# The order of TensorE's work inside one attention step: first half of the scores ahead of the turns

## The chip, the cores and the metric

The kernel runs on one core of a Trainium2 chip. The metric is the time of one execution on the device, in microseconds (us); lower is better. The engines are named as in the profile: PE is TensorE (PEld its weight loads), DVE is VectorE, ACT is ScalarE, POOL is GpSimd, SP is the queue that issues most transfers.

## The reference

Three stages follow one another, all in float32:

```python
# 1. attention with a top-32 mask: 4 batches, 8 heads, 576 rows, head size 64
scores = scale * np.matmul(q, k.transpose(0, 1, 3, 2))
kth = np.partition(scores, -32, axis=-1)[..., -32:-31]
scores = np.where(scores >= kth, scores, -1e9)
attn = np.exp(scores - scores.max(-1, keepdims=True))
x = (attn / (attn.sum(-1, keepdims=True) + 1e-9)) @ v      # 2304 tokens x 512
# 2. a gated layer, 512 -> 1536 -> 512
x = (x @ w_a * (x @ w_b)) @ w_out
# 3. eight experts 512 -> 1024 -> 512; each token goes to one, by cosine similarity
out[mask_e] = gate[mask_e] * (np.maximum(x[mask_e] @ w1[e], 0.0) @ w2[e])
```

## The kernel before, in words

**Tiles and parts.** Attention is cut into 144 tiles of 128 query rows by 576 keys. A part is a pair of heads of one batch and some of its rows, of 1, 4 or 5 tiles; there are 36 parts. The first part of a batch and head pair is called a lead part: it also brings in and turns its keys.

**One tile.** PE computes the scores in two halves of 288 columns (`scores`, matmul L373), and ACT copies each half from PSUM to `s` (L374). DVE finds the 32nd largest value of each row by four MAX8 (L394) and three MATCH_REPLACE8 (L397). ACT then makes a mask term (L406, into `z`), POOL subtracts it (L409), and ACT takes the exponential (L411). PE turns `z` by five transposes in two groups of 3 and 2 (`turn`, L428), and ACT copies both to `wt` (L431). When all tiles of a part are turned, the part's *mix* comes due: twenty matmuls with `v` (L469), then the spread of the row sums (L449); ACT evacuates both (L472 `xsb`, L457 `xR`). `finish` multiplies them on POOL (L481), splits the product in a high and a low piece (L227, L229), stores both (L491, L492) and, for the last head pair, raises `ready`, from which the groups of stage 2 become due.

**Steps.** A Python loop writes out, step by step, the order of PE, DVE, ACT and POOL. Each of these engines works its instructions in the order in which they are written; SP's transfers are ordered by priority. In step k, DVE's part is the top-32 search of tile k, and PE's part is the scores of tile k+2, the turn of tile k-4 (k-3 in the first 19 steps) and, if one is due, a mix. The softmax of tile k-2 begins (L406 and L409), and that of tile k-3 ends (L411).

**Slots.** PE's part of a step is five slots, filled by a tuple of generators: `tg` (one group of the turn at each call), `sg` (one half of the scores), `mg` (the due mix). After each slot, `run` lets a background go on for a share of time that is planned for the step; the background is stage 2, 256 tokens (a group) at a time: matmul L729, ACT copy L743 (`gab`), POOL products L663 (`gab`, `gl`) with an ACT copy between (`gh`), matmul L676. ACT and POOL instructions are written at fixed slot numbers, whatever generator stands there: the mask term at slot 1, the exponential at slot 3 (or at slot 2 while a mix is due), the subtraction at slot 4, and one *piece* (a stage of `finish`, or of the split of coming q and k, L227, L229, L302) at slots 2 and 4. A mix first works off all pieces that wait, and appends its own `finish` behind. Pieces are taken in the order in which they came.

```python
elif slot_ == (2 if mg is not none else 3):
    next(old if late else soft, None)
```

**After the slots**, up to two *flips* turn q and k of a coming part (L316), and ACT copies them to `qT` (L350) and `kT` (L334, L340). A planner (`level`) fixes how much background each step gets, from the step at which each group opens in the order before.

**Stages 2 and 3** end after the attention: the rest of the groups, then the experts (from about L1149 on), in which PE is fed by loads that were issued ahead.

Of the kernel before, what the change touches and what calls it, by code (L numbers as in the profile page):

```python
# [87 lines left out]
def fused_kernel(  # L88
# [118 lines left out]
    with ExitStack() as ph:  # L207
# [153 lines left out]
        def scores(t):  # L361
            o = t.o
            t.s = wk.tile([P, S], F32, name="s", bufs=SB)
            for j in range(2):
                p = ps.tile([P, 512], F32, name="tr", bufs=NTR)[:, :288]
                cs = slice(j * 288, (j + 1) * 288)
                if t.kind == 2:
                    terms = [(o.qm[:, a, h, :], o.kT[:, h, cs]) for h in range(2) for a in range(2)]
                else:
                    off = (2 * t.kind + t.c) * P  # L370
                    terms = [(o.qT[:, a, off : off + P], o.kT[:, t.kind, cs]) for a in range(2)]
                for i, (l, r) in enumerate(terms):
                    pe.matmul(p, l, r, start=(i == 0), stop=(i == len(terms) - 1))  # L373
                act.activation(t.s[:, cs], p, AF.Copy, scale=SCALE)  # L374
                yield 0.12 * len(terms)
# [37 lines left out]
        def turn(t):  # L413
            o = t.o
            for h in (0, 1) if t.kind == 2 else (t.kind,):
                if o.wt[h] is None:
                    o.wt[h] = wk.tile([P, 5, 320], F32, name="wt", bufs=WT)
            if t.kind == 2:
                dst = [(o.wt[h], slice(o.M, o.N), slice(h * 64, (h + 1) * 64)) for h in range(2)]
            else:  # L420
                dst = [(o.wt[t.kind], slice(t.c * P, (t.c + 1) * P), slice(0, P))]
            for c0, n5 in ((0, 3), (3, 2)):
                pt = ps.tile([P, 512], F32, name="tr", bufs=NTR)
                sl = slice(c0, c0 + n5)
                for i in range(n5):
                    cc = c0 + i
                    k0 = cc * P if cc < 4 else S - P
                    pe.transpose(pt[:, i * P : (i + 1) * P], t.w[:, k0 : k0 + P], ident)  # L428
                pv = pt[:, : n5 * P].rearrange("p (c j) -> p c j", c=n5)
                for th, w, src in dst:  # L430
                    act.activation(th[:, sl, w], pv[:, :, src], AF.Copy)  # L431
                yield 0.107 * n5
# [459 lines left out]
        def level(step):  # L892

            rates = []
            for w in opens + [NRW + TL]:
                if w > step:
                    rates.append((WORK * sum(x < w for x in opens) - spent[0]) / (w - step))
            return max(min(rates, default=STEP), 0.0) + SHARE
# [8 lines left out]
        def run(g):  # L907

            with tc.high_priority(offset=FG):
                c = next(g, None)  # L910
            if c is None:
                return False
            if now[0] >= 0:
                background(share[0])
            return True
# [12 lines left out]
        def piece():  # L928
            while pieces:
                with tc.high_priority(offset=FG):  # L930
                    if next(pieces[0], pieces) is not pieces:
                        return
                pieces.pop(0)
# [8 lines left out]
        for step in range(-AHEAD_L, NRW + TL + 5):  # L942
# [69 lines left out]
            tg = turn(live[i]) if 0 <= i < NRW else none  # L1012
            sg = scores(live[step + AHEAD_Q]) if 0 <= step + AHEAD_Q < NRW else none
            mg = mixes[0] if mixes else none
# [7 lines left out]
            if flips:  # L1022
                cost, n = cost + 0.44, n + 2
            share[0] = max((STEP0 if step < S0 else min(level(step), STEP)) - cost, 0.0) / max(n, 1)
            for slot_, g in enumerate((tg, sg, tg, mg, sg)):
                if g is not none and (not run(g) or step >= S0) and g is mg and mixes:
                    mixes.pop(0)
                    mg = none
                with tc.high_priority(offset=FG):
                    if slot_ == 1:  # L1030
                        next(soft, None)
                    elif slot_ == (2 if mg is not none else 3):
                        next(old if late else soft, None)
                    elif slot_ == 4 and late:
                        next(soft, None)
                    if slot_ in (0, 2, 4) and step >= 2:
                        conv.stage()
                    if slot_ == 3:
                        for _ in range(pace):
                            conv.open()  # L1040
                if slot_ in (2, 4):
                    piece()
# [408 lines left out]
```

## Time and profile before

| | |
|---|---|
| times of three runs, us | 1237.24, 1234.84, 1237.71 (median 1237.24) |
| the profiled execution's own time | 1235.7 us |
| its span from first to last instruction | 1233.9 us |
| PE busy, share of the span | 1132.0 us, 92% |
| DVE busy | 917.4 us, 74% |
| ACT busy | 822.3 us, 67% |
| POOL busy | 727.6 us, 59% |

The shares are means over stages with different limits: up to about 812 us the attention steps run, with DVE and PE both in use; afterwards DVE has little to do and PE works off the rest. "Idle before <-releaser" in a row is the time for which the engine stood still before that instruction, and what ended it.

### The profile page before, as it was taken

The page shows a single profiled execution, that of the slowest core. Times are in us where ns is not written, and L with a number is a line of the kernel's source. Part 1 is how long each engine was busy: PE and PEld are TensorE (multiplying, and loading weights), DVE is VectorE, ACT ScalarE, POOL GpSimd, SP SyncE. Part 2 cuts the span into 40 slices and gives each one's busy share as a digit, 9 for nine tenths or more (in the row PEclk, how much of TensorE's full clock was granted, in tenths as well). Part 3 has the DMA queues.
Part 4 walks back from the last instruction along what each step waited for, and adds up shares of the span by engine and source line. Part 5 has one row for each costly group of instructions (what it writes and reads, how often), then busy time and mean ns, then how long its engine had stood idle before and what let it go on. Part 6 is the DMA issues. An engine that isn't in the chain of part 4 may idle for free. (4 is left out here: it accounts for less than half of the span.)

```text
span 1233.9 us, 23912 instructions
## 1 busy us (share of the span) xinstructions
PE 1132.0 (92%) x8124; PEld 980.1 (79%) x8125; DVE 917.4 (74%) x2015; ACT 822.3 (67%) x1970; POOL 727.6 (59%) x1195
## 2 busy tenths in 40 slices
PE   5676789999999998999999999989999989999996
PEld 4445567787897886888888888877998869999995
DVE  8999999999999997999999999940210225655540
ACT  5877879888778886788878777763532435554441
POOL 5655688777776876776788677664455420322211
PEclk8778999999999998999999999999999999999998
DMA  7334567667785766767666667657988145565530
GB/s 237 121 122 145 195 199 249 218 222 214 223 249 172 191 209 205 213 193 227 185 196 190 203 199 223 204 171 234 338 264 243 65 154 180 203 216 197 179 103 28
DMA packets 129200, 240.05 MB, mean 195 GB/s; under 512 B 24896, under 2 KB 74176, under 8 KB 129074
## 3 DMA queue, kind: packets, MB, share of 16 engines
q1 hardware_dynamic: 125170, 228.74, 59.2%
q0 software_dynamic: 3904, 9.75, 2.1%
q8 instruction: 65, 1.06, 0.4%
q14 instruction: 61, 0.50, 0.1%
HBM read 198.38 MB, written 40.31 MB: 193 GB/s over the span
## 5 line engine op out<-in xcount | busy, mean ns | idle before, releaser
L394 DVE MAX8 t<-y 128x8 f32<-128x576 f32 x432 | 311.8, 749 | 2.6
L409 POOL TENSOR_TENSOR z<-s,z 128x576 f32<-128x576 f32 x144 | 206.4, 1434 | 84.1 <-ACT z L406 77.9
L397 DVE MATCH_REPLACE8 y<-t,y 128x576 f32<-128x576 f32 x288 | 214.0, 743 | 0.0
L729 PE MATMUL ab<-xg,wab 128*128 128x256 f32 x1398 | 209.7, 289 | 3.1 <-DMA wab<-wab_d 1.8
L729 PEld LDWEIGHTS ab<-xg,wab 128*128 128x128 f32 x1398 | 182.9, 189 | 6.7 <-DMA wab<-wab_d 2.2
L428 PE MATMUL tr<-ident,z 128*128 128x128 f32 x720 | 134.0, 285 | 46.1 <-ACT z L411 42.6
L729 PE MATMUL ab<-raw,wab 128*128 128x256 f32 x1152 | 171.5, 288 | 3.4 <-DMA wab<-wab_d 2.0
L729 PEld LDWEIGHTS ab<-raw,wab 128*128 128x128 f32 x1152 | 150.0, 189 | 6.5 <-ACT gab L743 1.9
L431 ACT ACTIVATE wt<-tr 128x384 f32<-128x384 f32 (+2 forms) x320 | 128.2, 412 | 40.2 <-PE tr L428 38.9
L374 ACT ACTIVATE s<-tr 128x288 f32<-128x288 f32 x288 | 118.0, 410 | 48.6 <-PE tr L373 34.5
L428 PEld LDWEIGHTS tr<-ident,z 128*128 128x128 f32 x720 | 89.0, 145 | 64.9 <-ACT z L411 54.4
L676 PE MATMUL x<-wo,gh 128*128 128x512 f32 x432 | 136.3, 397 | 0.0
L1157 POOL DMA_INDIRECT out_dram<-o,ids x24 | 31.6, 1318 | 172.7 <-ACT o L1156 121.9
L1104 DVE TENSOR_TENSOR u<-raw,u 128x1024 fp32r<-128x1024 f32 x64 | 76.2, 1221 | 75.7 <-ACT u L1103 48.1
L373 PE MATMUL tr<-kT,qT 128*128 128x288 f32 x512 | 124.0, 327 | 5.0 <-ACT s L374 3.2
L411 ACT ACTIVATE z<-z,bi 128x576 f32<-128x576 f32 x144 | 112.2, 779 | 0.3 <-POOL z L409 0.3
L394 DVE MAX8 t<-s 128x8 f32<-128x576 f32 x144 | 107.1, 744 | 6.5 <-ACT s L374 6.5
L406 ACT ACTIVATE z<-s,bi 128x576 f32<-128x576 f32 x144 | 111.4, 773 | 0.2 <-DVE bi L399 0.2
L663 POOL TENSOR_TENSOR gl<-gab,gh 128x256 fp32r<-128x256 f32 x108 | 80.9, 749 | 51.5 <-ACT gh L663 47.9
L663 POOL TENSOR_TENSOR gab<-gab 128x256 f32<-128x256 f32 x108 | 82.2, 761 | 47.5 <-ACT gab L743 41.7
L397 DVE MATCH_REPLACE8 y<-t,s 128x576 f32<-128x576 f32 x144 | 107.0, 743 | 0.0
L373 PEld LDWEIGHTS tr<-kT,qT 128*128 128x128 f32 x512 | 86.9, 201 | 15.2 <-ACT s L374 3.6
(201 smaller groups left out, 2246.7 us busy)
## 6 DMA issues: line engine op xcount, KB each, us to landing
wab<-wab_d SPq DMA_DIRECT2D x192, 512.0 KB
raw<-in_moe_w_dram SPq DMA_DIRECT2D x28, 1024.0 KB
wab_d<-wab SPq DMA_DIRECT2D x24, 512.0 KB
kT<-kT_d SPq DMA_DIRECT2D x20, 576.0 KB
vs<-in_v_dram SPq DMA_DIRECT2D x36, 256.0 KB
kT_d<-kT SPq DMA_DIRECT2D x16, 576.0 KB
raw<-in_moe_w_a_dram SPq DMA_DIRECT2D x12, 512.0 KB
raw<-in_moe_w_b_dram SPq DMA_DIRECT2D x12, 512.0 KB
```

Of the source, the lines that this page charges most:

```text
L373: pe.matmul(p, l, r, start=(i == 0), stop=(i == len(terms) - 1))
L374: act.activation(t.s[:, cs], p, AF.Copy, scale=SCALE)
L394: dve.max(v, cur)
L397: dve.match_replace(out=rest, in_to_replace=v, in_values=cur, imm_value=LOWEST)
L406: act.activation(t.w, t.s, AF.Relu, bias=t.bi[:, 1:2], scale=-HUGE)
L409: pool.tensor_tensor(t.w, t.s, t.w, op=OP.subtract)
L411: act.activation(t.w, t.w, AF.Exp, bias=t.bi[:, 0:1], accum_out=t.o.sm[:, t.slot : t.slot + 1])
L428: pe.transpose(pt[:, i * P : (i + 1) * P], t.w[:, k0 : k0 + P], ident)
L431: act.activation(th[:, sl, w], pv[:, :, src], AF.Copy)
L663: pend.pop(0)[1]()
L676: pe.matmul(px[t], g[:, ts], wo[:, w, f], start=(f == 0 and i == 0), stop=(f == NF - 1 and i == 2))
L729: pe.matmul(ps_[i], wt[:, a, c, :], xg[x][:, c, :], start=(j == 0 and f not in begun), stop=(j == len(terms) - 1),)
```

## The change

The tuple that fills the five slots is written in another order:

```diff
-            for slot_, g in enumerate((tg, sg, tg, mg, sg)):
+            for slot_, g in enumerate((sg, tg, mg, tg, sg)):
```

Before: turn (3 transposes), scores 1, turn (2 transposes), mix, scores 2. After: scores 1, turn (3), mix, turn (2), scores 2. Nothing is added or left out. What is tied to slot numbers stays at its number, so it changes places with what stands there:

- A mix stands at slot 2 and not 3. Its `finish` is appended one slot sooner, and the piece of slot 2 is then its first stage.
- In a step with a mix, `mg` is cleared in slot 2 (from step 16 on), so that the exponential comes at slot 3, behind the mix and the second group of the turn. Without a mix it stays where it was, behind the second group.
- Scores 1 comes directly behind the flips and the background that end the step before.

## Rows read from the trace of the kernel before

**Rows 1.** Windows: stretch, busy us (instructions) of PE, PEld, DVE, ACT, POOL; clock, DMA.

```profile
0.00:105.00 105.00, 64.28 (x345) 45.27 (x346) 99.95 (x239) 76.15 (x174) 59.67 (x86) 0.83 0.47 149
105.00:250.00 145.00, 128.72 (x798) 97.05 (x799) 141.47 (x289) 122.67 (x276) 109.88 (x130) 0.95 0.65 216
250.00:812.00 562.00, 543.18 (x4213) 471.28 (x4211) 538.34 (x1251) 445.66 (x1165) 416.83 (x737) 0.99 0.68 206
...
1050.00:1200.00 150.00, 150.00 (x1115) 148.88 (x1114) 84.22 (x120) 73.98 (x119) 38.91 (x32) 1.00 0.54 183
```

**Rows 2.** Waits of DVE, 250 to 812 us: total us, times, longest.

```profile
DVE rc L439 <- POOL rc L437: 14.2, 9, 2.4
DVE t L394 <- ACT s L374: 5.7, 7, 3.7
```

**Rows 3.** Waits of PE, 250 to 812 us.

```profile
PE tr L428 <- ACT z L411: 6.1, 10, 1.2
PE x L676 <- POOL gl L663: 6.0, 2, 4.2
```

**Rows 4.** Waits of PE, 0 to 105 us.

```profile
PE tr L428 <- ACT z L411: 23.8, 14, 2.7
```

**Rows 5.** Timeline, 309 to 313 us: start, us, instruction; turn and q copy.

```profile
310.88 0.55 PE L428 MATMUL tr<-ident,z 128*128 128x128 f32 x3
311.01 0.60 ACT L350 ACTIVATE qT<-tr 128x512 fp32r<-128x512 f32 x1
```

**Rows 6.** Timeline, 693 to 700 us: the same place, a later part.

```profile
693.42 1.10 ACT L350 ACTIVATE qT<-tr 128x512 fp32r<-128x512 f32 x2
...
694.43 0.49 PE L428 MATMUL tr<-ident,z 128*128 128x128 f32 x3
```

**Rows 7.** Timeline, 643 to 650 us: a step with a mix.

```profile
644.03 0.38 PE L428 MATMUL tr<-ident,z 128*128 128x128 f32 x2
...
644.34 3.06 PE L469 MATMUL tr<-wt,vs 128*64 128x320 f32 x20
...
645.31 0.38 ACT L431 ACTIVATE wt<-tr 128x256 f32<-128x256 f32 x1
...
645.57 0.78 ACT L411 ACTIVATE z<-z,bi 128x576 f32<-128x576 f32 x1
...
646.24 0.21 ACT L411 ACTIVATION_READ_ACCUMULATOR z<-z,bi 128x1 f32 x1
...
647.33 0.92 PE L449 MATMUL tr<-ident,rc 128*64 128x128 f32 x12
...
648.11 1.44 POOL L409 TENSOR_TENSOR z<-s,z 128x576 f32<-128x576 f32 x1
...
648.18 0.74 PE L729 MATMUL ab<-xg,wab 128*128 128x256 f32 x4
648.30 0.44 ACT L457 ACTIVATE xR<-tr 128x320 f32<-128x320 f32 x1 [0.41 <-PE tr L449]
...
648.76 0.43 PE L373 MATMUL tr<-kT,qT 128*128 128x288 f32 x2
...
649.23 0.41 ACT L374 ACTIVATE s<-tr 128x288 f32<-128x288 f32 x1 [0.49 <-PE tr L373]
```

**Rows 8.** Groups by line, 250 to 812 us: count, busy us, mean ns, idle before.

```profile
L411 ACT ACTIVATE z<-z,bi 128x576 f32<-128x576 f32 x104 | 80.9, 778 | 0.0
...
L394 DVE MAX8 t<-s 128x8 f32<-128x576 f32 x105 | 78.1, 744 | 5.7 <-ACT s L374 5.7
...
L481 POOL TENSOR_TENSOR xsb<-xsb,xR 128x320 f32<-128x320 f32 (+2 forms) x26 | 19.2, 739 | 21.0 <-ACT xR L457 20.9
...
L472 ACT ACTIVATE xsb<-tr 128x320 f32<-128x320 f32 (+2 forms) x26 | 10.1, 387 | 15.8 <-PE tr L469 15.8
```

**Rows 9.** Timelines near 480 and 808 us: searches that waited for scores.

```profile
480.53 0.76 DVE L394 MAX8 t<-s 128x8 f32<-128x576 f32 x1 [3.73 <-ACT s L374]
...
807.92 0.76 DVE L394 MAX8 t<-s 128x8 f32<-128x576 f32 x1 [0.31 <-ACT s L374]
```

## The prediction

> **What bounds the kernel now.** I read first the windows by stretch, then the waits of DVE and of PE, then the timeline around the places where the change puts something else. The windows [rows 1] show three regimes within the attention steps and after them. Up to 105 us DVE is busy 99.95 of 105 us and PE 64.28: DVE alone sets the pace. From 105 to 250 us it is the same, 141.47 of 145. From 250 to 812 us both are nearly full, PE 543.18 and DVE 538.34 of 562 us. After the attention steps PE is full by itself (150.00 of 150 us from 1050 on), and the change does not touch that part.
>
> The middle stretch therefore decides. There DVE stands still 23.7 us (562 less 538.34); 14.2 us of it is for a row sum that POOL delivers late, 5.7 us for scores that come late [rows 2]. Both are work that PE, ACT and POOL do in PE's step, so DVE waits exactly when PE's step lags. PE's own waits there are few: 6.1 us in ten waits for the exponential `z`, which the turn needs, and 6.0 us in two waits for POOL's `gl` at the end of a group [rows 3]. The reader is to see that neither engine has more than some 20 us to give in this stretch, and that they are tied: PE that loses a microsecond shows it as a DVE wait once the scores have no reserve left. That was so at three places, the first at 480 and the last at 808 us, with one near 705 us between them [rows 9].
>
> PE waits longest for `z` early, 23.8 us in 14 waits before 105 us [rows 4]. That is worth nothing: DVE is 95% busy there and PE has 40 us to spare.
>
> **The change part by part.** No instruction and no transfer is added or removed; PE, DVE, ACT and POOL do the same work in another order, so all terms are waits.
>
> *Turn one place later.* The first transposes now stand behind scores 1 (two matmuls, 0.43 us [rows 7]) and the background that follows. The ten waits for `z` last at most 1.2 us and 0.61 us on the mean [rows 3]; 0.43 us plus one background portion, some 0.6 to 0.7 us, covers nearly all of them (a portion is 0.74 us in [rows 7]). Term: -6.1 us, with 0 as the other end, if DVE sets the pace anyhow.
>
> *Scores 1 one place earlier.* It now stands directly behind the flips, whose result it needs when a lead part begins. Before, the turn lay between. In [rows 5] PE is free at 310.88 us, and the copy of q ends at 311.61; with 0.1 us for the signal scores 1 would have waited 0.83 us. In [rows 6] it is 694.43 against 694.52: 0.19 us. I read the nine such places between these two times in the same way: 0.83, 1.04, 0.82, 0.35, 1.53, 0.68, 0.71, 0.43 and 0.19, together 6.6 us. Term: +6.6 us, with 0 as the other end where the scores' reserve hides it. Earlier ones stand under DVE [rows 1].
>
> *The mix one place earlier, the exponential behind it.* This is an edit that the diff does not show as such. In a mix step of before, ACT takes the exponential at 645.57 us, while PE is busy for 3 us with the mix and ACT would have nothing else [rows 7]; ACT then stands idle for the mix, 15.8 us in 26 steps [rows 8]. After the change the exponential (0.78 and 0.21 us) and the copy of the second group (0.38 us) come behind the mix, and so in front of the copy of scores 2: 1.37 us of ACT, of which PE's scores 2 hides 0.43. With 0.1 us for the signal scores 2 lands about 1.0 us later in each of the 26 mix steps. What waits for it is DVE's search two steps on. A fixed delay costs only where the reserve is gone, and then once, as DVE is later from there: three such places [rows 9], so +3.0 us. The ends are 0 (the reserve holds) and the price of the slower rival below.
>
> The next step's turn needs that exponential. Counted from the end of the sums' matmuls (648.25 in [rows 7]), PE has 0.74 of background, 0.38 of turn, 0.43 and 0.43 of scores, and 0.7 of background in front of it, 2.7 us; ACT has `z` ready after 0.74, 0.38, 0.1, 0.38 and 0.78, some 2.4 us. So the turn is just covered. Without a portion of background there it would wait up to 0.45 us.
>
> *POOL.* The product of `finish` (0.74 us [rows 8]) stood behind the subtraction in POOL's order and now stands in front of it, and waits for `xR`. In [rows 7] the subtraction would begin after 648.35 (`xR` one turn group of 0.38 us sooner) plus 0.74, so some 1 us later than its 648.11. Behind it are the background's products. I put this at nothing, because the exponential never waited for the subtraction in this stretch (0.0 idle [rows 8]) and comes most of a step later; if that cover were gone, it would cost 0.74 us in 26 steps, 19 us [rows 8].
>
> *Groups.* `finish` ends one piece place sooner, so `ready` rises in the step before and each later group opens one step earlier than the planner assumes. That can spare the two waits for `gl` at a group's end, when no next group was open to fill in: between -6.0 and 0 us [rows 3]. Both also have POOL's full queue in them, so I take -1.0. SP issues the stores of `finish` half a step sooner; the queue has the same transfers.
>
> **Sum.** -6.1 + 6.6 + 3.0 - 1.0 = +2.5 us, on the profiled execution's 1235.7 us: 1238.2 us. Its time is 1.5 us under the median of the runs, 1237.24, so this is 1 us above that median. About 0.3%, 3.7 us, is what a measurement of this kernel can tell from no change; the forecast is no change that can be measured.
>
> **The rivals.**
>
> *Faster: the waits for `z` go, and nothing takes their place.* For it: only 7 of 105 searches waited for their scores [rows 2, 8], so a copy of q that comes 0.7 us late need not reach DVE. Against it: the reserve is gone in three places [rows 9]. Time: 1235.7 - 6.1 - 1.0 = 1228.6 us.
>
> *Slower: the exponential behind the mix.* It decides from the point at which the background between scores 2 and the next turn is shorter than about 0.4 us, which is likely in steps with a mix, as the planner leaves them little background. Then each of the 26 mix steps hands 0.45 us on, 11.7 us: 1247.4 us. For it: ACT loses the only time in which it had nothing to do. Against it: in [rows 7] there was a portion of 0.7 us.
>
> *No effect, DVE alone sets the pace.* DVE is busy 95.8% of the stretch (538.34 of 562 [rows 1]), PE's weight loads only 84% (471.28), while they are at 99% (148.88 of 150) where PE is clearly the bound. If PE thus has room, each wait that comes or goes on PE is taken up by it: 1235.7 us. The Trainium skill, page "Perfetto Trace Analysis", section "Identifying the Most-Contended Engine", speaks for this rival: matmul occupancy misleads, and TensorE's headroom is to be judged by the busy share of its weight loads. By that rule the sum would be 0 and not +2.5. The rows only half agree: with 16% of room by weight loads, DVE still waited 19.9 us for what PE's step brings late [rows 2].
>
> **How the numbers follow.** Forecast 0.31, no effect 0.12, faster 0.30, slower 0.27. The time is the forecast's, 1238.2 us; its own range is 1234 to 1242, since its two large terms each lie between 0 and 6.6. The range for all is 1228 to 1247 us: it reaches to either rival and leaves out about a third of each. Faster by over 0.3%: 0.30. Within: 0.31 + 0.12, less 0.02 for the forecast's upper edge, 0.41. Slower: 0.27 + 0.02, 0.29.
>
> **What would show it.** In the waits of PE between 250 and 812 us, the turn's wait for `z` should fall from 6.1 us to under 2, and scores (L373) waiting for the copy of q (L350) should appear with 4 to 7 us. In a mix step ACT should show the exponential behind `xR`, and the copy of scores 2 about 1 us behind its matmul instead of 0.04. DVE's waits for scores should rise from 5.7 us to some 8. The early waits for `z`, 23.8 us, should shrink by a quarter or more (0.43 us each) without moving the first 105 us. The prediction is wrong if DVE's waits of 14.2 and 5.7 us fall together, which would mean that PE's step as a whole gained; if POOL's product of `finish` holds back the background so far that PE waits for `gl` more than twice; or if a group's earlier opening fills a hole of several microseconds that the waits do not show.

## The result, and the profile after

The kernel after takes 1254.7 us (median of 4 runs, 1252.99 to 1256.78) against 1236.04 us (4 runs, 1232.94 to 1237.71): a ratio of 1.0145, 95% interval 1.0119 to 1.0172. The change makes the kernel some 18 us slower. The forecast, 1238.2 us with a range of 1228 to 1247, was wrong. The profiled execution took 1253.7 us, with a span of 1252.0.

The page of the kernel after: span, then busy time and its share by engine.

```profile
span 1252.0 us, 23867 instructions
PE 1139.1 (91%) x8124; PEld 983.7 (79%) x8125; DVE 918.6 (73%) x2015; ACT 815.2 (65%) x1970; POOL 726.1 (58%) x1195
```

Busy times are those of before within 1%, POOL's too (726.1 against 727.6 us). What came is standing still. The windows of the kernel after (the columns of [rows 1]):

```profile
0.00:105.00 105.00, 71.61 (x373) 49.17 (x375) 100.14 (x235) 77.80 (x179) 60.10 (x87) 0.89 0.48 152
105.00:250.00 145.00, 121.20 (x725) 89.33 (x724) 136.25 (x282) 114.68 (x255) 104.48 (x124) 0.93 0.60 200
250.00:812.00 562.00, 530.84 (x4104) 461.79 (x4103) 524.36 (x1217) 428.97 (x1140) 406.01 (x715) 0.99 0.67 203
1050.00:1200.00 150.00, 149.83 (x1136) 148.38 (x1135) 87.32 (x123) 76.78 (x122) 35.63 (x30) 1.00 0.58 196
```

For DVE the first 105 us are as before (100.14 us busy against 99.95). From 105 to 250 us DVE, which sets the pace there, loses 5.2 us (136.25 against 141.47), and from 250 to 812 us 14.0 (524.36 against 538.34). The granted clock has hardly changed behind 105 us: 0.93 and 0.99 against 0.95 and 0.99. The last search of the attention steps shows the same. This is its start in the timeline of the kernel after:

```profile
831.98 0.74 DVE L394 MAX8 t<-s 128x8 f32<-128x576 f32 x1
```

In the kernel before it began at 807.92 [rows 9]: the attention steps lose 24.1 us. What stands behind that search takes 6.0 us less (1252.0 - 831.98 against 1233.9 - 807.92), and 18.1 us are left.

Waits of DVE and of PE in the attention steps of after, 250 to 836 us (total, times, longest):

```profile
DVE rc L439 <- POOL rc L437: 23.7, 15, 3.0
DVE t L394 <- ACT s L374: 15.1, 9, 5.5
```

```profile
PE x L676 <- POOL gl L663: 7.8, 5, 2.3
PE ab L729 <- DMA xg<-xl_d: 7.1, 1, 7.1
PE tr L428 <- ACT z L411: 5.0, 5, 3.3
PE tr L373 <- ACT qT L350: 4.0, 6, 1.3
```

Against [rows 2] and [rows 3], both of DVE's waits rose (14.2 and 5.7 before), and PE waits five times for `gl`, and once for 7.1 us for a transfer of the group's input. DVE's standing still carries the loss. From 105 us to the start of the last search, the windows of the kernel before and of the kernel after are:

```profile
105.00:807.92 702.92, 667.82 (x4980) 564.76 (x4981) 675.73 (x1529) 565.89 (x1435) 523.90 (x862) 0.98 0.68 208
105.00:831.98 726.98, 672.02 (x4979) 568.59 (x4978) 676.73 (x1534) 557.89 (x1432) 523.94 (x866) 0.98 0.65 202
```

DVE has the same work in both, 675.73 and 676.73 us, and stands still 27.2 and 50.2 us: 23.1 of the 24.1 us. Its wait for row sums rises there from 14.2 to 25.2 us, that for scores from 5.4 to 15.1.

The waits that changed most are those of POOL and of ACT, which delay DVE only through what they deliver. Kernel after, 250 to 836 us:

```profile
POOL xsb L481 <- ACT xR L457: 69.4, 24, 6.4
```

```profile
ACT s L374 <- POOL z L409: 45.8, 45, 2.8
```

POOL's product of `finish` waited 20.9 us for `xR` before [rows 8]; now it is 69.4. ACT's copies of scores, which in the whole execution of before waited 6.2 us in 7 waits for POOL's subtraction, wait 45.8 us in 45.

The timeline of one mix step shows how. First the kernel before:

```profile
725.96 3.06 PE L469 MATMUL tr<-wt,vs 128*64 128x320 f32 x20
...
726.25 0.78 ACT L406 ACTIVATE z<-s,bi 128x576 f32<-128x576 f32 x1
...
727.11 1.41 POOL L409 TENSOR_TENSOR z<-s,z 128x576 f32<-128x576 f32 x1 [1.20 <-ACT z L406]
...
729.91 0.44 ACT L457 ACTIVATE xR<-tr 128x320 f32<-128x320 f32 x1 [0.41 <-PE tr L449]
...
730.43 0.88 POOL L481 TENSOR_TENSOR xsb<-xsb,xR 128x320 f32<-128x320 f32 x1 [1.90 <-ACT xR L457]
```

The same mix in the kernel after:

```profile
739.31 3.06 PE L469 MATMUL tr<-wt,vs 128*64 128x320 f32 x20
739.75 0.41 ACT L374 ACTIVATE s<-tr 128x288 f32<-128x288 f32 x1 [1.10 <-POOL z L409]
...
740.42 0.78 ACT L406 ACTIVATE z<-s,bi 128x576 f32<-128x576 f32 x1
...
742.30 0.92 PE L449 MATMUL tr<-ident,rc 128*64 128x128 f32 x12
...
743.27 0.44 ACT L457 ACTIVATE xR<-tr 128x320 f32<-128x320 f32 x1 [0.41 <-PE tr L449]
743.34 0.52 PE L373 MATMUL tr<-kT,qT 128*128 128x288 f32 x2
...
743.78 0.88 POOL L481 TENSOR_TENSOR xsb<-xsb,xR 128x320 f32<-128x320 f32 x1 [4.07 <-ACT xR L457]
743.90 0.77 ACT L411 ACTIVATE z<-z,bi 128x576 f32<-128x576 f32 x1
...
744.66 0.40 ACT L374 ACTIVATE s<-tr 128x288 f32<-128x288 f32 x1
...
744.78 1.45 POOL L409 TENSOR_TENSOR z<-s,z 128x576 f32<-128x576 f32 x1
```

Before, the subtraction of the step ran at 727.11, as soon as the mask term was there and while PE was in the mix; only then did POOL wait for `xR`. After, the product stands in front, POOL stands still for 4.07 us until mix, spread and copy are done, and the subtraction, whose mask term was there at 741.20, begins at 744.78. Over the 26 mix steps of steps 40 to 140, worked out from the starts and ends in the traces, the subtraction begins 0.87 us after its mask term ends before, and 3.29 us after.

### The profile page after: what moved, and what is told of

Its sections match the earlier page's. It is cut to its first block, busy times and chain, and to the rows that moved or that the text cites. A ratio compares the mean times of both kernels' runs of the same rounds, so it can differ in the third digit from the quotient of the medians.

```text
span 1252.0 us, 23867 instructions
## 1 busy us (share of the span) xinstructions
PE 1139.1 (91%) x8124; PEld 983.7 (79%) x8125; DVE 918.6 (73%) x2015; ACT 815.2 (65%) x1970; POOL 726.1 (58%) x1195
## 5 line engine op out<-in xcount | busy, mean ns | idle before, releaser
L729 PE MATMUL ab<-xg,wab 128*128 128x256 f32 x1398 | 213.2, 291 | 9.9 <-DMA xg<-xl_d 7.1
L374 ACT ACTIVATE s<-tr 128x288 f32<-128x288 f32 x288 | 119.3, 414 | 65.0 <-POOL z L409 48.5
L428 PE MATMUL tr<-ident,z 128*128 128x128 f32 x720 | 131.0, 286 | 33.0 <-ACT z L411 31.1
```

Source lines behind the costliest of these rows:

```text
L729: pe.matmul(ps_[i], wt[:, a, c, :], xg[x][:, c, :], start=(j == 0 and f not in begun), stop=(j == len(terms) - 1),)
```

## The experiments

Ratios are to the kernel before, run beside each kernel on the same chip, with the 95% interval. "Wait" is the time from the end of the mask term to the start of the subtraction, the mean over those 26 mix steps.

### The tuple, part by part

Scores 1 in front, everything else as before:

```diff
-            for slot_, g in enumerate((tg, sg, tg, mg, sg)):
+            for slot_, g in enumerate((sg, tg, tg, mg, sg)):
```

> Only the scores moved: scores 1, turn (3), turn (2), mix, scores 2; the mix, the exponential, the pieces and the opening of groups stay as before the change. Ring theory: most of the loss is here, 1247 to 1254 us, with ACT's copies of scores waiting more than 30 us for POOL's subtraction. POOL order and exponential: about the kernel before, 1234 to 1240 us. The copies of q that come too late for scores 1 (4 to 9 us of waits of PE) are in this kernel under every theory.

Measured: 1235.71 us, 1.0029 [1.0009, 1.0049]. This part alone is a small loss, about 3.6 us. In the waits of PE (105 to 835 us) the turn's wait for `z` falls from 18.8 to 11.3 us, and scores wait 7.5 us for the copy of q (0.3 us before).

The mix one place earlier, turn and scores 1 as before:

```diff
+            for slot_, g in enumerate((tg, sg, mg, tg, sg)):
```

> Only the mix moved: turn (3), scores 1, mix, turn (2), scores 2. POOL order: the product of finish stands in front of the subtraction, groups open one step early, and most of the loss is here, 1246 to 1254 us, with POOL waiting over 60 us for xR. Exponential behind the mix: also 1246 us or more, as it is moved here too. Ring: 1234 to 1241 us.

Measured: 1252.99 us, 1.0168 [1.0137, 1.0199]; wait 3.43 us. The loss comes with the mix's place, and with what is tied to it: the pieces of `finish`, and the exponential.

### POOL's product

The kernel after, with no piece in the slot in which a mix stands, so that the product is back behind the subtraction:

```diff
             for slot_, g in enumerate((sg, tg, mg, tg, sg)):
+                due = g is mg and g is not none
...
-                if slot_ in (2, 4):
+                if slot_ in (2, 4) and not due:
                     piece()
```

> The changed kernel, but the piece of slot 2 is left out in a step with a mix, so that finish begins at slot 4 behind the subtraction, and groups open at the step of before. POOL order: the loss goes, 1236 to 1243 us, and POOL's waits for xR fall from 89 to about 31 us. Ring and exponential: above 1248 us. Of the 7.1 us that PE waits for the load of xl_d near 789 us, nothing is left if the early opening is its cause.

Measured: 1240.48 us, 1.0063 [1.0038, 1.0088]; wait 0.70 us. More than half of the loss is gone. In its waits (105 to 835 us) the copies of scores wait 19.4 us for the subtraction:

```profile
ACT s L374 <- POOL z L409: 19.4, 22, 1.4
```

The other way round, the kernel before with the product in front of the subtraction and nothing else changed:

```diff
+            held = False
             for slot_, g in enumerate((tg, sg, tg, mg, sg)):
+                held = held or (g is mg and g is not none and late)
+                if slot_ == 4 and held:
+                    piece()
...
-                if slot_ in (2, 4):
+                if slot_ in (2, 4) and not held:
```

> The kernel before, with one thing changed: from step 19 on, in a step with a mix, the product of finish is written directly behind the mix, in front of scores 2 and of POOL's subtraction, as the change has it. PE's and ACT's order and the opening of groups stay. If POOL that stands in front of a mix is a cost of its own: 1.006 to 1.010, with POOL waiting some 60 us or more for xR and DVE's waits (20 us between 250 and 812 us before) up by 8 us or more. If it costs only together with the exponential behind the mix: 0.999 to 1.003.

Measured: 1248.25 us, 1.0138 [1.0121, 1.0155]; wait 3.81 us. This one step costs 17 us by itself, more than was expected. The waits of POOL and of ACT in this kernel, 105 to 830 us:

```profile
POOL xsb L481 <- ACT xR L457: 93.0, 28, 7.4
```

```profile
ACT s L374 <- POOL z L409: 34.8, 33, 2.4
```

And its window from 105 us to the last search, in which DVE stands still 41.0 us (27.2 before), 22.4 us of it for row sums and 6.4 for scores:

```profile
105.00:821.90 716.90, 669.82 (x4981) 565.43 (x4981) 675.92 (x1534) 564.86 (x1439) 523.88 (x862) 0.98 0.65 204
```

Is it the wait for `xR`, or the 0.74 us of work ahead of the subtraction? In the kernels that follow, a stand-in does not wait for `xR`: it multiplies ready values into `xh`. The attention output is then not scaled by the row sums. It is called the product that waits for nothing, though it can wait for a store that still reads `xh`.

```diff
-            pool.tensor_tensor(o.xsb[:, :N], o.xsb[:, :N], o.xR[:, :N], op=OP.mult)
+            vc = o.vs.rearrange("p h c d -> p h (c d)")[:, :, : N // 2]
+            pool.tensor_tensor(o.xh.bitcast(F32)[:, :N].rearrange("p (h n) -> p h n", h=2), vc, vc, op=OP.mult)
```

The control, on the kernel before in its own order:

> Control: the kernel before, its order unchanged, with the same product that waits for nothing. Both theories: 0.998 to 1.002; its distance from 1 is what leaving the wait out is worth by itself, and is to be taken off the other two.

Measured: 1232.83 us, 0.9996 [0.9984, 1.0008].

On the kernel before with the product first:

> The kernel before with the product of finish ahead of the subtraction, but a product that waits for nothing: it multiplies two ready values (v by itself) into xh, so the attention output is not scaled by the row sums. POOL's work and its order are those of the run that put the product first and took 1.0138. Theory (the wait): POOL stood still behind the product for xR, 93.0 us in 28 waits, and everything behind it in POOL's order stood too; without the wait only 0.74 us in a mix step is left, about a quarter of the 2.9 us by which the subtraction came later, so 0.0 to 0.4% of time: 1.000 to 1.004. Rival (the place): any work ahead of the subtraction is the price, and the time stays at 1.010 or above.

Measured: 1233.53 us, 1.0000 [0.9986, 1.0013]; wait 1.21 us. The order is that of the kernel that took 1.0138; the wait for `xR` is gone, and with it the whole loss. What is left of waiting, 6.4 us in two waits for stores out of `xh`, stands at the parts of one tile. A mix step of this kernel in the timeline (the product is L482, as the edit adds a line):

```profile
647.49 0.72 POOL L482 TENSOR_TENSOR xh<-vs 128x320 f32<-128x320 f32 x1
647.84 0.44 ACT L457 ACTIVATE xR<-tr 128x320 f32<-128x320 f32 x1 [0.41 <-PE tr L449]
648.18 0.21 POOL L408 TENSOR_SCALAR bi<-t 128x1 f32<-128x1 f32 x1
648.35 1.43 POOL L409 TENSOR_TENSOR z<-s,z 128x576 f32<-128x576 f32 x1
```

The product no longer waits for `xR`, which here ends at 648.28, and the copies of scores wait for the subtraction about as in the kernel before (105 to 830 us):

```profile
ACT s L374 <- POOL z L409: 8.1, 8, 2.1
```

DVE stands still 25.0 us up to the last search, against 41.0 with the wait; its wait for row sums is 12.8 us and that for scores 4.5:

```profile
105.00:807.30 702.30, 668.62 (x4981) 566.23 (x4982) 677.33 (x1537) 563.80 (x1435) 519.18 (x862) 0.98 0.66 208
```

On the kernel after:

> The kernel after with the same product that waits for nothing (the attention output is not scaled by the row sums). Theory (the wait): as good as taking the product back behind the subtraction, 1.003 to 1.008, and the copies of scores wait for the subtraction some 10 to 20 us and not 48.5. Rival (the place, or the exponential behind the mix): 1.012 or above.

Measured: 1245.95 us, 1.0096 [1.0072, 1.0120]; wait 1.29 us. A third of the loss went, less than expected: by itself the wait is not all that the change costs. (Here the stand-in waits 9.0 us in three waits for stores out of `xh`.)

The product later still, in the kernel before (pieces behind the mix held to the next step):

```diff
+            held = False
...
+                held = held or (g is mg and g is not none and late)
...
-                if slot_ in (2, 4):
+                if slot_ in (2, 4) and not held:
```

> The kernel before, the other way round: in a step with a mix finish does not begin at slot 4, but at slot 2 of the next step, and it ends in the same step as before, so that groups open as before. POOL then hardly waits for xR (21 us in 16 waits between 250 and 812 us before). If POOL that stands in front of a mix is a cost of its own, this gains: 0.995 to 0.999. If not: 1.000 to 1.002.

Measured: 1241.05 us, 1.0068 [1.0046, 1.0090]. Later is a loss as well, which neither theory expected; its cause was not followed.

### The exponential behind the mix

The kernel before, with the exponential at slot 3, so behind the mix:

```diff
-                    elif slot_ == (2 if mg is not none else 3):
+                    elif slot_ == (2 if mg is not none and not late else 3):
```

> The kernel before, with one thing changed: from step 19 on the exponential is written at slot 3 also in a step with a mix, so that it stands behind the mix on ACT. The price of this alone. My prediction's term is +3.0 us (1.0 us at three places), its slower rival 11.7 us: ratio 1.002 or 1.009. If it is free: 0.998 to 1.001.

Measured: 1251.80 us, 1.0137 [1.0105, 1.0168], more than either figure expected. PE's waits of this kernel, 105 to 835 us:

```profile
PE tr L428 <- ACT z L411: 25.0, 32, 2.9
```

With the turn first in the next step, the turn waits for the exponential; in the same stretch of the kernel before it did so for 18.8 us in 19 waits. These 6.2 us are not the 17 that the edit costs; through what the rest comes is not shown.

In the kernel after, the exponential put ahead of the mix again:

```diff
+                if g is mg and g is not none and late:
+                    with tc.high_priority(offset=FG):
+                        next(old, None)
```

> The changed kernel, with only the exponential written ahead of the mix again, as before the change. If the two orders add up (the product worth 0.8%, the exponential 0.2% where scores 1 covers it): 1.011 to 1.014. If the exponential behind the mix is needed for the loss: 1.003 to 1.006.

Measured: 1251.36 us, 1.0176 [1.0142, 1.0211]. No gain while the product waits in front, and not the sum of the two parts that was expected. With the product back behind the subtraction as well (this edit and that of the kernel with 1.0063):

> The run with the piece left out of slot 2 (1.0063), and the exponential written ahead of the mix again, as before the change. What is left of the change is the order of scores 1, first turn, mix and second turn on PE. If the rest of 0.6% is the exponential behind the mix: like the run with only the scores moved, 1.003, or less. If it is the second turn behind the mix: 1.005 to 1.008 still.

Measured: 1238.38 us, 1.0040 [1.0018, 1.0062]; against 1.0063 without it, a difference inside the intervals. And with the product in front that waits for nothing:

> The kernel after with the product that waits for nothing (1.0096 with that alone; the attention output is not scaled by the row sums) and the exponential ahead of the mix again. Theory (what is left is the exponential behind the mix, as it was 1.0137 alone): 1.001 to 1.005. Rival (the exponential costs nothing behind scores 1, as 1.0063 against 1.004 said): 1.007 to 1.011.

Measured: 1239.36 us, 1.0042 [1.0026, 1.0059], against 1.0096 without it. Here the exponential's place is worth 0.5%.

The kernel after with the product behind the subtraction and waiting for nothing:

> The kernel after with the product behind the subtraction, and a product that waits for nothing. Control for the run that only moved the product back (1.0063): if POOL's pieces one place sooner, with no wait of the product, are what is left, 1.002 to 1.007; if it is neither the pieces nor the wait, 1.008 to 1.011.

Measured: 1238.87 us, 1.0035 [1.0021, 1.0050]; wait 0.72 us. Three repairs that share only the order of the tuple end at 1.0035 to 1.0042, and scores 1 in front alone took 1.0029.

### The groups that open sooner

The kernel after, each group opened one step later, as before:

```diff
-                w = step + (D0 if done == 0 else RD)
+                w = step + 1 + (D0 if done == 0 else RD)
```

> The changed kernel, with each group opened one step later than finish allows, which is the step of the kernel before. The product of finish stays in front of POOL's subtraction. If the early opening (the two 128-token-wide loads of a group come one step sooner after the stores, and PE meets the load of xl_d with 7.1 us of wait near 789 us) is the cost: 1236 to 1244 us. If POOL's order is the cost: 1246 to 1254 us, with POOL still waiting over 80 us for xR.

Measured: 1251.67 us, 1.0159 [1.0120, 1.0199]. The same edit with a product that waits for nothing:

> The kernel after with the product that waits for nothing and each group of the gated layer opened one step later, as in the kernel before. If the groups' early opening and the transfer that PE waited for carry what is left: 1.002 to 1.006. If not: 1.007 to 1.011.

Measured: 1241.18 us, 1.0067 [1.0045, 1.0089], against 1.0096; the intervals overlap, so a gain is not shown.

The kernel with the product behind the subtraction (1.0063), and one piece more at slot 4 of a mix step, so that groups open as early as in the kernel after:

```diff
+            held = False
...
+                held = held or due if slot_ else False
+                if slot_ == 4 and held:
+                    piece()
```

> The changed kernel, with the product of finish behind the subtraction in slot 4 (as in the run with the piece left out of slot 2, 1.0063 of the kernel before), but with two pieces there, so that finish catches up and groups open one step early, as after the change. Early opening: 1246 to 1254 us, and the 7 us of wait for xl_d near 789 us come back. POOL's order: 1237 to 1244 us, like that run.

Measured: 1238.94 us, 1.0053 [1.0034, 1.0071]. The early opening does no harm that can be measured, although the wait for the transfer comes with it (5.7 us here, 7.1 in the kernel after).

### The ring of score buffers

ACT's copies of scores wait for the subtraction because `s` has five buffers, and a copy writes the one that the subtraction still reads. The kernel after with six, and single buffers for two small tiles to make room:

```diff
-SB = 5
+SB = 6
...
-            r = wk.tile([P, 5, D], F32, name="qr")
+            r = wk.tile([P, 5, D], F32, name="qr", bufs=1)
...
-            o.xsb = wk.tile([P, 320], F32, name="xsb")
+            o.xsb = wk.tile([P, 320], F32, name="xsb", bufs=1)
```

> The changed kernel with six buffers for the scores tile s and not five (room for it comes from one buffer each, not two, for xsb and for the raw q). Three theories. Ring: scores 1 of tile k+2 now comes first in step k and writes the buffer of tile k-3, which POOL's subtraction, written at the end of step k-1, still reads; ACT's copy waits for it (48.5 us in 49 waits over the whole kernel after the change, 6.2 us in 7 waits between 105 and 820 us before). If that is the cost, these waits vanish and the time falls by 12 to 18 us, to 1237 to 1243 us. POOL order: the product of finish stands in front of the subtraction and waits for the mix; then the copy's waits vanish, but the time stays above 1249 us. Exponential behind the mix: the time stays above 1249 us too, and the turn's waits for z stay.

Measured: 1253.65 us, 1.0168 [1.0129, 1.0208]. No gain. The control, the same three lines in the kernel before:

> The control for the run with six buffers for s: the kernel before with the same three sizes of buffers (s six, xsb one, raw q one). If the single buffers hid a gain of the sixth there, this is slower than before by 8 us or more, above 1.006; if the ring of s truly is no cost, it is within 0.998 to 1.003.

Measured: 1239.22 us, 1.0057 [1.0038, 1.0077]. The two single buffers cost something themselves. If that cost is the same in both kernels, the sixth buffer is worth about 0.3% in the kernel after (1.0145 + 0.0057 - 1.0168), within the intervals. In the waits of ACT with six buffers (105 to 835 us), the copies' waits for the subtraction, 48.5 us with five, are gone, and those of another customer of POOL rise from 3.1 us:

```profile
ACT gh L663 <- POOL gab L663: 9.8, 13, 2.7
```

## Why the prediction was wrong

**The step that failed is the one named *POOL*, put at nothing.** The order was seen; the price was wrong in two places. That POOL's delay reaches DVE stood in my own reading: 14.2 us of DVE's standing still was for a row sum that POOL delivers late [rows 2].

The first is the size of the delay. I took it from one step [rows 7], in which the subtraction began at 648.11 and would have moved to about 649.1, 1 us. But that is the step of a lead part, in which POOL still works on coming keys: its mask term had ended at 645.42, 2.69 us earlier. Over 26 mix steps the subtraction of before begins 0.87 us after its mask term, while PE has most of the mix still to do. In front of it now stands a product that needs the mix, the spread and its copy, and the mean delay is 2.4 us (3.29 less 0.87), not 1.

The second is the cover. I named the exponential, which never waited for the subtraction. That held: in the 26 steps of the kernel after it begins 2.46 us after the subtraction ends (4.15 before). But the exponential is only one customer. What stood still was POOL's whole queue. The next copy of scores needs the buffer that the subtraction reads, for which ACT already waited 5.7 us in six waits between 250 and 812 us before, and the background's products stand behind it. The copies' waits rose to 45.8 us, and on ACT they stand ahead of the exponential. I priced the 0.74 us of the product's work and not its wait. The runs split the two: with the wait 1.0138, with the work alone 1.0000 (control 0.9996). My bound for a lost cover, 19 us, was near the 17 us measured, by a mechanism that it did not describe.

**Scores 1 and the turn** make +0.5 us by my terms (+6.6 and -6.1); with both moved 3.6 us were measured (1.1 to 6.0), so somewhat more. In the kernel after PE waits 4.0 us in six waits for the copy of q, inside the forecast of 4 to 7. The turn's waits for `z` fell only from 6.1 to 5.0 us, and not under 2. Before 105 us they fell from 23.8 us [rows 4] to 17.2, by 28% where a quarter or more was forecast, and that moved nothing.

**The exponential behind the mix** I costed at +3.0 us, with a rival of 11.7. As told, the copy of scores 2 comes later behind its matmuls: 744.66 against 743.86 in the step shown, 0.8 us where I said 1.0. The condition that I gave, "just covered" by scores 1 and a background portion, is borne out on one side: with the turn first, the same exponential costs 1.0137; with scores 1 in front and the product back behind, 0.2% that the intervals don't tell from nothing. With the product ahead of the subtraction it depends on the wait: 0.5% if the product waits for nothing (1.0096 against 1.0042), nothing if it waits (1.0145 against 1.0176). So the slower rival, 1247.4 us, named the sign but not the cause: putting this step right alone brings nothing back.

**Groups**: -1.0 us is too little to be told from nothing (1.0053 against 1.0063), but the two waits for `gl` that it was to spare became five. The early opening is not the loss either.

**No effect, DVE alone** (0.12) is refuted, and so is faster. Weight loads take 82% of the stretch from 250 to 812 us in the kernel after (461.79 of 562) against 84% before [rows 1]. The Trainium skill, page "Perfetto Trace Analysis", section "Identifying the Most-Contended Engine", judges TensorE's headroom by this share, and by the matmul work done against the peak. The 18% of room did not take up the new waits: DVE, busy 93% of this stretch (524.36 of 562 us), waits for what PE, ACT and POOL deliver, and the time rose by 18 us.

Of the signs that I had named for a wrong forecast one appeared: PE waited for `gl` five times (7.8 us) and not twice. DVE's waits for scores rose to 15.1 us and not 8, and those for row sums by 9.5 us (14.2 to 23.7).

**What the parts add up to, and what is open.** In the kernel after, the product's place carries the largest part: 0.8% (1.0145 to 1.0063), of which 0.5% goes with the wait alone (1.0096). What is left with it repaired, 0.4 to 0.6%, is near the 0.3% of scores 1 in front. The parts do not add: product first and exponential behind cost 1.4% each on the kernel before, and together with scores 1 in front also 1.4%. Two things stay open. The first is why, with a product that does not wait for `xR`, the pieces cost 0.6% one slot sooner (1.0035 against 1.0096) where the exponential stands behind the mix, and nothing where it does not. The second is the way from POOL's delay to DVE. Where it arrives is seen: DVE waits longer for row sums and for scores, with the product first alone 22.4 and 6.4 us, and 12.8 and 4.5 without its wait. The row sums wait hardly longer in POOL's queue itself: over the parts of the same 26 mix steps their add on POOL begins 1.65 us after the last exponential that it needs in the kernel after, and 1.47 before. That is 4.7 us in all, of 9.5 us by which DVE's wait rose (14.2 to 23.7), so at least a good part seems to come with exponentials that end later against DVE's search. That the copies of scores hold the exponentials up on ACT fits this, but is argued and not shown: with a sixth score buffer the copies' waits went, others on POOL rose, and the time stayed.

No version was faster than the kernel before; its order of product and subtraction was better than the place ahead and the place behind.

## What to carry to other kernels

When an instruction is moved ahead of others on an engine that works in order, price its wait and not its work, and apply it to everything queued behind it, not only to the next consumer that comes to mind. Read the reserve from all steps of the kind, not from the one that is shown: the one I read was the one in which the engine was already late, so the delay looked like 1 us where the mean was 2.4. An engine that is busy 59% can cost 1.4% of the time without one more busy microsecond, and its row in a table of busy shares will hardly change (58% here). What shows it is the standing still of the engine that sets the pace, and what ended it.

## What the runs showed that was not expected

The wait-free product of 320 columns took 0.72 us and the one that multiplies `xsb` with `xR` 0.88 us, for as many elements of the same type; the wait-free one reads a single tile for both inputs. Why was not tried. It stands in the control too, and so does not bear on the comparison of 1.0000 with 0.9996.
